# A down-projection in seven products instead of eight, for two of three token blocks

## The chip, the cores and the metric

The kernel runs on one NeuronCore of a Trainium2 chip. The metric is the device time of one execution in microseconds (us). The engines are TensorE (PE: matmuls, with its weight loads as PEld), VectorE (DVE), ScalarE (ACT), GpSimd (POOL) and SyncE (SP), which here only issues DMAs. Matmuls write to PSUM, which has eight banks of 2 KB per partition; a [128 x 512] fp32 tile fills one bank.

## The reference

Sliding-window attention over 4 x 8 heads gives x of 2304 tokens by 512. Two feed-forward layers follow:

```python
a = x @ w_a                       # 512 -> 1536
b = x @ w_b
x = (a * b) @ w_out               # first layer's down-projection, 1536 -> 512
h = x @ w_in                      # 512 -> 2048
g = np.where(h >= 1, h, np.where(h <= -1, 0.0, (h + 1) ** 2 / 4.0))
out = g @ w_out2                  # second layer's down-projection, 2048 -> 512
```

## The kernel before

**Numbers in two parts.** A float32 operand is split into a rounded part (hi) and what is left (lo), both in the type fp32r; a product is three matmuls, hi by hi, hi by lo and lo by hi. ACT makes hi by a copy (L924), DVE makes lo by a subtraction (`minus`, L153).

**Visits.** The tokens lie in three blocks of 768 (`BW`); half a block is 384 (`QW`). After the attention and the first part of the first layer, the work goes in visits (layer, block): a short plain one, then (1,0), (1,1), (1,2), (2,0), (2,1), (2,2). In a visit of the second layer the loop runs over eight pairs of 128-wide feature chunks. For each pair the up-projection is done in seven products of a Strassen scheme (`seven_steps`, L975; q = 0 to 6), six matmuls of 128 x 384 each, into the two banks of the pool `ps_mm`. `bend7` turns their sums into the two chunks of g (`bend`: two ACT passes, a DVE pass at L1018, then hi and lo).

**Down-projection.** For each chunk `down2_pieces` makes six pieces, one for each 128 tokens: three matmuls of 128 x 512 (L1157) that add into one PSUM bank. The six banks (two of the pool `ps_acc`, four of `ps_acc2`) stay open over all sixteen chunks, so that DVE and ACT read them only once, at the end of the visit (L161, L159), before the DMA to `out`.

**Order.** TensorE's order is as the code is written (`MANUAL`). After each product q, `hook` calls `after`, which issues pieces by a rate of 12/7 per hook (`state["credit"]`), while more than `HOLD` = 3 pieces are queued: pieces of a pair run among the products of the next pairs. The other engines' order comes from the framework's scheduler, with the reads of PSUM raised by `urgent()`.

**Weights.** The weights come as 64-bit words. Background jobs (`background`, rates and limits in `BG`) decode them (`words`), form Strassen's combinations for the up-projections (`seven_job`), split them (`staged`) and store them in DRAM. Visits load them from there by SP into 14 tiles of 512 KB (`fill`, L940). `x7_second` prepares the combinations of x for a visit of the second layer, while the visit before it runs.

```python
for k, (m, i) in enumerate(((gh, 0), (gh, 1), (gl, 0))):
    nc.tensor.matmul(
        v["acc"][n], m[:, ss], w[:, i], start=first and k == 0, stop=last and k == 2,
    )
```

Of the kernel before, what the change touches and what calls it, by code (L numbers as in the profile page):

```python
# [26 lines left out]
def attention_and_two_ffns(  # L27
# [631 lines left out]
    for f in range(0, NF2, 2):  # L659
        late += [("ii", f), ("p", f), ("p", f + 1)]  # L660
# [46 lines left out]
    def staged(key, j, src):  # L707
# [12 lines left out]
        minus(V, t[:, 1, :n], src, t[:, 0, :n])  # L720
# [36 lines left out]

    def run(jobs):

        try:  # L760
            return next(jobs[0]) != "no room"
        except StopIteration:
            jobs.popleft()
            return True

    def next_w():
        if not jobs_w and late:
            key = late.popleft()
            jobs_w.append((seven_job if key[0] in ("ab", "ii") else plain_job)(key))
# [27 lines left out]
    def x7_first(b, where):  # L797
# [4 lines left out]
        if where == "memory":  # L802
            parked[b] = {q: dram.tile([P, 2, 2, QW], F32, name=f"t_{b}{q}") for q in (2, 3, 6)}
# [3 lines left out]
        def split(q, c, src):  # L807
# [14 lines left out]
            if q != 4 and where == "memory":  # L822
                nc.sync.dma_start(parked[b][q][:, :, c], t[:, :, :QW].bitcast(F32))
# [37 lines left out]
    def x7_second(b, where):  # L861
# [3 lines left out]
        turned[2, b] = {q: t_tile(where) for q in (2, 3, 6)}  # L865
# [6 lines left out]

        for c in range(2):
# [4 lines left out]
            part = lambda q: [turned[2, b][q][:, z, c] for z in range(2)]  # L878
# [6 lines left out]
            yield from split(*part(3), t1)  # L885
            yield from split(*part(2), t2)
# [5 lines left out]
            yield from split(*part(6), t1)  # L892
# [34 lines left out]
    def fill():  # L927

        while plan:
# [5 lines left out]
            if (key, j) not in wd or room() <= (v < 4):  # L935
# [143 lines left out]
    def down1_pieces(v, f, g):  # L1079
# [29 lines left out]
        return [lambda n=n: go(n) for n in (0, 1, 4, 2, 3, 5)]  # L1109
# [36 lines left out]
    def down2_pieces(v, f, g):  # L1146
# [156 lines left out]
```

## Time and profile before

| what | value |
|---|---|
| median of 3 runs (lowest, highest) | 976.31 us (973.74, 978.48) |
| profiled execution, its span | 976.94 us, 975.2 us |
| PE busy, DVE, ACT, POOL (share of the span) | 96%, 67%, 56%, 13% |
| visits by time in the span (us) | (1,0) 317 to 410, (1,1) to 502, (1,2) to 594.5, (2,0) to 720, (2,1) to 845.4, (2,2) to 971.4 |

Busy time of PE is no measure of its rate, since matmuls overlap in it; the rate is read from the distance between the starts of matmuls that follow one another. The same holds for short instructions of DVE: the listed time of one includes its write at the end, which the next one overlaps.

### The profile page before, as it was taken

The page shows a single profiled execution, that of the slowest core. Times are in us where ns is not written, and L with a number is a line of the kernel's source. Part 1 is how long each engine was busy: PE and PEld are TensorE (multiplying, and loading weights), DVE is VectorE, ACT ScalarE, POOL GpSimd, SP SyncE. Part 2 cuts the span into 40 slices and gives each one's busy share as a digit, 9 for nine tenths or more (in the row PEclk, how much of TensorE's full clock was granted, in tenths as well). Part 3 has the DMA queues.
Part 4 walks back from the last instruction along what each step waited for, and adds up shares of the span by engine and source line. Part 5 has one row for each costly group of instructions (what it writes and reads, how often), then busy time and mean ns, then how long its engine had stood idle before and what let it go on. Part 6 is the DMA issues. An engine that isn't in the chain of part 4 may idle for free.

```text
span 975.2 us, 17548 instructions
## 1 busy us (share of the span) xinstructions
PE 940.9 (96%) x6172; PEld 866.6 (89%) x6172; DVE 651.8 (67%) x1567; ACT 544.4 (56%) x1305; POOL 127.9 (13%) x279
## 2 busy tenths in 40 slices
PE   5999999899999999999999999999999999999998
PEld 4889888889999999999989999989988898989887
DVE  6698788784764989785677667899874333444343
ACT  6778676664433454343444435888775545545453
POOL 4567444344100000000000000000000000000000
PEclk9899999999999999999999999999999999999999
DMA  9966787830435888799868998876876553265521
GB/s 217 187 137 164 219 206 198 217 106 2 154 139 196 318 308 315 279 351 343 268 229 322 387 363 276 312 243 217 300 266 198 188 180 108 82 214 181 184 76 65
DMA packets 172103, 212.44 MB, mean 218 GB/s; under 512 B 92400, under 2 KB 129776, under 8 KB 172016
## 3 DMA queue, kind: packets, MB, share of 16 engines
q1 hardware_dynamic: 168576, 208.44, 66.3%
q10 hardware_dynamic: 3440, 2.88, 0.9%
q8 instruction: 49, 0.80, 0.3%
q14 instruction: 38, 0.31, 0.1%
HBM read 147.06 MB, written 64.23 MB: 217 GB/s over the span
## 4 chain that ended last, share of the span: by engine, by line
PE 71%; DVE 4%; DMA 3%; issue 1%; ACT 0%; SPq 0%; POOL 0%; DVEq 0%; POOLq 0%
PE mm L975 33%; PE acc L1157 20%; PE acc L1096 10%; PE mm L1065 2%; DMA xf<-xf 1%; PE ps_s L331 1%; PE ps_o L395 1%; PE acc L621 1%; PE mm L572 1%; DMA w<-in_moe_w_b_dram 1%; PE mm L574 1%; PE mm L573 1%; DVE x L829 1%; DMA e<-w_b 0%; PE ps_t L363 0%
## 5 line engine op out<-in xcount | busy, mean ns | idle before, releaser
L1157 PE MATMUL acc<-ws,gh 128*128 128x512 f32 x444 | 138.1, 392 | 0.0
L975 PE MATMUL mm<-xt,ws 128*128 128x384 f32 x612 | 123.4, 336 | 0.3 <-DVE a L916 0.3
L975 PEld LDWEIGHTS mm<-xt,ws 128*128 128x128 f32 x612 | 107.4, 188 | 7.3 <-DVE a L916 0.9
L975 PE MATMUL mm<-z,ws 128*128 128x384 f32 x480 | 97.0, 337 | 0.5 <-DVE h L916 0.5
L975 PEld LDWEIGHTS mm<-z,ws 128*128 128x128 f32 x480 | 86.0, 188 | 7.6 <-DVE h L916 0.8
L1157 PEld LDWEIGHTS acc<-ws,gh 128*128 128x128 f32 x444 | 81.6, 188 | 9.3
L1018 DVE SCALAR_TENSOR_TENSOR c<-h,c 128x384 f32<-128x384 f32 x96 | 53.1, 555 | 53.9 <-ACT c L1017 53.7
L1157 PE MATMUL acc<-ws,gl 128*128 128x512 f32 x222 | 88.1, 397 | 0.0
L916 DVE TENSOR_TENSOR h<-mm,s 128x384 f32<-128x384 f32 x72 | 40.0, 556 | 71.0 <-PE mm L975 70.8
L924 ACT CAST gh<-c 128x384 fp32r<-128x384 f32 x96 | 47.8, 512 | 68.2 <-PE acc L1157 65.8
L1016 ACT ACTIVATE c<-h,half 128x384 f32<-128x384 f32 x96 | 59.0, 616 | 26.7 <-DVE gl L153 16.0
L352 POOL TENSOR_SCALAR s<-s,ssum 128x192 f32<-128x192 f32 (+2 forms) x144 | 69.1, 492 | 29.5 <-DVE ssum L347 20.9
L341 ACT ACTIVATE s<-s,nmax 128x192 f32<-128x192 f32 (+2 forms) x144 | 62.6, 439 | 15.5 <-DVE nmax L337 15.1
L153 DVE TENSOR_TENSOR gl<-c,gh 128x384 fp32r<-128x384 f32 x96 | 52.0, 555 | 28.8 <-ACT gh L924 28.5
L975 PE MATMUL mm<-x,ws 128*128 128x384 f32 x348 | 70.4, 336 | 0.4 <-ACT s L996 0.2
L1096 PE MATMUL acc<-gh,ws 128*128 128x512 f32 (+1 forms) x224 | 65.7, 337 | 0.0
L975 PEld LDWEIGHTS mm<-x,ws 128*128 128x128 f32 x348 | 61.7, 188 | 4.0 <-ACT s L996 0.9
L331 PE MATMUL ps_s<-kt,diag 128*128 128x192 f32 (+2 forms) x288 | 62.7, 339 | 2.5 <-DVE nmax L337 1.0
L512 ACT ACTIVATE e<-w 128x512 f32<-128x512 f32 x68 | 45.4, 671 | 35.1 <-DMA w_a<-e 6.3
L924 ACT CAST gh<-a 128x384 fp32r<-128x384 f32 x56 | 28.3, 513 | 55.4 <-DVE a L1004 37.8
L514 ACT ACTIVATE up<-w 128x512 uint32<-128x512 uint32 x68 | 45.9, 675 | 21.5 <-DVE e L525 9.1
L572 PE MATMUL mm<-x,w 128*128 128x256 f32 x192 | 57.2, 302 | 0.2
(126 smaller groups left out, 2223.6 us busy)
## 6 DMA issues: line engine op xcount, KB each, us to landing
ws<-w_ii SPq DMA_DIRECT2D x55, 512.0 KB, 4.2
ws<-w_ab SPq DMA_DIRECT2D x37, 512.0 KB, 6.4
ws<-w_p SPq DMA_DIRECT2D x33, 512.0 KB, 3.7
w<-in_moe_w_out_dram SPq DMA_DIRECT2D x28, 512.0 KB, 4.8
w_ab<-wb SPq DMA_DIRECT2D x24, 512.0 KB, 2.9
w_ii<-wb SPq DMA_DIRECT2D x24, 512.0 KB, 3.5
w<-in_moe_w_in_dram SPq DMA_DIRECT2D x16, 512.0 KB, 4.9
w_p<-wb SPq DMA_DIRECT2D x16, 512.0 KB, 5.3
```

Source lines behind the costliest of these rows:

```text
L153: eng.tensor_tensor(out_, a, hi.bitcast(F32), ALU.subtract)
L331: nc.tensor.matmul(ps[:, z, c : 3 * D], qd[:, i - q0 // D, :], kt[:, (i - 2) * D + c - k0 : (i + 1) * D - k0], start=True, stop=True,)
L341: nc.scalar.activation(at(z, i), at(z, i), AF.Exp, bias=nmax[:, z : z + 1], scale=-1.0, accum_out=ssum[:, z : z + 1],)
L352: ENG[E_N[2 * b + (m >= 2)][z]].tensor_scalar(at(z, i), at(z, i), ssum[:, z : z + 1], 1.0, ALU.mult, ALU.mult)
L514: nc.scalar.activation(up, lo, AF.Copy, scale=2.0**-29)
L572: nc.tensor.matmul(ps, w[:, 0, cs], xh[c], start=(c == 0), stop=False)
L924: nc.scalar.copy(hi[:, t_], src)
L975: nc.tensor.matmul(ps, w[:, k, cs], operand(here, q, ci, m), start=q in (0, 1, 3) and ci + n == 0, stop=ci == 1 and n == 2, skip_group_che ...
L1016: nc.scalar.activation(c, h, AF.Relu, bias=half, scale=0.5)
L1018: V.scalar_tensor_tensor(c, h, 1.0, c, ALU.max, ALU.min)
L1096: nc.tensor.matmul(dst, w[:, i, cs], m[:, t_], start=first and k == 0 and (n < NC or c % 2 == 0), stop=last and k == 2 and (n < NC or c % ...
L1157: nc.tensor.matmul(v["acc"][n], m[:, ss], w[:, i], start=first and k == 0, stop=last and k == 2,)
```

## The change

In the visits (2,1) and (2,2) (`D7`), seven of the eight pairs are projected down by Strassen's scheme, for two chunks by two halves of the tokens by two halves of the 512 outputs. The last pair of each visit is done by the eight plain products, which also close the sums.

- `bend14` takes the place of `bend7`: the curve is applied in place to four halves (a11, a12, a21, a22), POOL forms four combinations of them (`E_C` = 'P'), and all seven operands are split into hi and lo (four halves of 384, twice, were split before).
- `down7_pieces` takes the place of `down2_pieces`: 21 pieces of three matmuls of 128 x 256, three (128 tokens each) for each of seven products, in `ORDER` 0, 6, 3, 1, 2, 5, 4. Products 1, 5 and two thirds of 6 stay in four open PSUM banks; 0, 2, 3, 4 and the rest of 6 go through the two banks of `ps_acc` and are added to sums in SBUF after each pair (`evict`: by ACT in the first pair of a visit, else by DVE). A piece counts 4/7, so three are issued in a hook.
- `close7_pieces` does the last pair: 12 pieces of six matmuls of 128 x 256, then the sums and four DMAs of 384 KB. Before it POOL combines the four sums in SBUF (`E_W`).
- `second_job` makes the weights of the second down-projection: the plain ones as before, and two more tiles for each pair with four combinations (`p7`), by POOL (`E_PC`), stored in DRAM. All weight work ends before (2,1) begins (`last_places`), and `BG` is set so that it runs earlier.
- The x combinations for (2,2) go through DRAM, as those of (1,1) do, and `last_places` gives the freed SBUF to the sums and the operands.

```diff
-    BG = [(3, 2, 24), (3, 1, 24), (1.5, 1, 19), (2, 1, 12), (3, 1, 0), (3, 1, 0), (2, 1, 0)]
+    BG = [(3, 2, 16), (3, 1, 14), (2, 1, 11), (2, 1, 7), (4, 1, 0), (3, 1, 0), (2, 1, 0)]
...
+    def second_job(key):
...
+        yield from staged(("p", f), 0, w[:, 0:2].rearrange("p a n -> p (a n)"))
+        yield from staged(("p", f + 1), 0, low)
+        for dst, i, j in ((t1, b12, b11), (t2, b22, t1), (t3, b22, b12), (t4, b21, t2)):
+            ENG[E_PC].tensor_tensor(dst, i, j, ALU.subtract)
+            yield
+        for j in range(2):
+            yield from staged(("p7", f), j, w[:, 2 + 2 * j : 4 + 2 * j].rearrange("p a n -> p (a n)"), ENG[E_PC])
...
+        def curve(h):
+            c = later["act"].tile([P, QW], F32, tag="c", name="c", bufs=CB)
+            nc.scalar.activation(c, h, AF.Relu, bias=half, scale=0.5)
+            nc.scalar.activation(c, c, AF.Square)
+            V.scalar_tensor_tensor(h, h, 1.0, c, ALU.max, ALU.min)
...
+                elif q == 5:
+                    sub(a22, a21, a22, ALU.add)
+                    sub(a21, a11, a21)
+                    sub(a11, a22, a11)
+                    split(3, a22)
+                    split(4, a21)
+                    split(2, a11)
+                elif q == 6:
+                    split(1, a12)
+                    sub(a12, a12, a11)
+                    split(5, a12)
...
+    ORDER = (0, 6, 3, 1, 2, 5, 4)
...
+        def evict(dst, ps):
+            with urgent(PRI_E):
+                if first:
+                    ecopy(E_F[len(dst.shape) - 2], dst, ps)
+                else:
+                    plus(dst, ps, dst)
...
+            if m < 2:
+                if q in (1, 5, 6):
+                    ps, opens, closes = v["acc"][q], first and m == 0, False
+                else:
+                    if m == 0:
+                        state["bank"] = ps_acc.tile([P, 2, HW], F32, tag="acc", name="acc")
+                    ps, opens, closes = state["bank"], m == 0, True
+                dst = ps[:, m]
+            elif q in (1, 5):
+                dst, opens, closes = v["rest"][:, q // 5], first and q == 1, False
+            else:
+                ps = ps_acc.tile([P, 2, HW], F32, tag="acc", name="acc")
+                dst, opens, closes = ps[:, 0], True, True
+            ss = slice(m * P, (m + 1) * P)
+            for n, (a, b) in enumerate(((0, 0), (0, 1), (1, 0))):
+                nc.tensor.matmul(
+                    dst, g[a][:, ss], w[:, b], start=opens and n == 0, stop=closes and n == 2,
+                    skip_group_check=True,
+                )
+            if m == 1 and q not in (1, 5, 6):
+                evict(v["sum"][q][:, 0:2], state["bank"])
+            if m == 2 and q not in (1, 5):
+                evict(v["sum"][q][:, 0 if q == 6 else 2], dst)
...
+        return [(4 / 7, lambda q=q, m=m: go(q, m)) for q in ORDER for m in range(3)]
```

TensorE before, in (2,2): two hooks of a pair (`mm` are the products of the up-projection, `acc_10184` and the following the six open banks).

```order
L975 MATMUL mm_10941<-xt_8900,ws_10756 128x384 x6
L1157 MATMUL acc_10185<-ws_10683,gh_10841 128x512 x2
L1157 MATMUL acc_10185<-ws_10683,gl_10842 128x512
L1157 MATMUL acc_10186<-ws_10683,gh_10841 128x512 x2
L1157 MATMUL acc_10186<-ws_10683,gl_10842 128x512
L975 MATMUL mm_10993<-xt_8901,ws_10756 128x384 x6
```

TensorE now, in (2,2), after q = 0, 1 and 2 of a pair: `acc_11593` and `acc_11613` are product 4 of the pair before (two thirds, then one third), `acc_11618` is product 0 of the next, all three in the two banks of `ps_acc`.

```order
L1346 MATMUL acc_10837<-ws_11182,go_11341 128x256 x6
L1025 MATMUL mm_11574<-z2_9035,ws_11407 128x384 x3
L1025 MATMUL mm_11574<-z3_9036,ws_11407 128x384 x3
L1346 MATMUL acc_10839<-ws_11182,go_11341 128x256 x3
L1346 MATMUL acc_11593<-ws_11129,go_11307 128x256 x6
L1025 MATMUL mm_11552<-xt_10459,ws_11409 128x384 x6
L1346 MATMUL acc_11613<-ws_11129,go_11307 128x256 x3
L1346 MATMUL acc_11618<-ws_11260,goh_11392 128x256 x2
L1346 MATMUL acc_11618<-ws_11260,gol_11393 128x256
```

Between two products of the up-projection stand now nine matmuls of 128 x 256 where three or six of 128 x 512 stood. In every pair `acc_11618` is the place where a bank is wanted again soonest: it is that of `acc_11593`.

VectorE before, in (2,2), one pair in a row: three sums of products (`h0`, `h1`), four ends of the curve (`c`), four lo parts (`gl`).

```order
L916 TENSOR_TENSOR h0_10574<-mm_10567,s1_10559 128x384
L153 TENSOR_TENSOR gl_10500<-c_10502,gh_10499 128x384
L153 TENSOR_TENSOR gl_10500<-c_10541,gh_10499 128x384
L1018 SCALAR_TENSOR_TENSOR c_10578<-h0_10574,c_10578 128x384
L916 TENSOR_TENSOR h1_10631<-mm_10552,s1_10615 128x384
L153 TENSOR_TENSOR gl_10576<-c_10578,gh_10575 128x384
L916 TENSOR_TENSOR h0_10574<-mm_10608,s2_10600 128x384
L1018 SCALAR_TENSOR_TENSOR c_10635<-h1_10631,c_10635 128x384
L1018 SCALAR_TENSOR_TENSOR c_10653<-h0_10574,c_10653 128x384
L153 TENSOR_TENSOR gl_10576<-c_10653,gh_10575 128x384
L1018 SCALAR_TENSOR_TENSOR c_10674<-h1_10631,c_10674 128x384
```

VectorE now, in (2,2), around the same place as TensorE's piece (`sum4` and `sum0` are the evictions of products 4 and 0, `go` lo parts of operands).

```order
L1236 SCALAR_TENSOR_TENSOR h1_11464<-h1_11464,c_11528 128x384
L966 TENSOR_TENSOR sum2_10832<-acc_11561,sum2_10832 128x256
L166 TENSOR_TENSOR gol_11500<-h1_11464,goh_11499 128x384
L166 TENSOR_TENSOR gol_11500<-h0_11386,goh_11499 128x384
L966 TENSOR_TENSOR h0_11581<-mm_11574,s1_11559 128x384
L166 TENSOR_TENSOR go_11505<-h0_11386,go_11505 128x384
L966 TENSOR_TENSOR sum4_10834<-acc_11593,sum4_10834 128x512
L166 TENSOR_TENSOR go_11532<-h1_11464,go_11532 128x384
L1236 SCALAR_TENSOR_TENSOR h0_11581<-h0_11581,c_11583 128x384
L966 TENSOR_TENSOR sum4_10834<-acc_11613,sum4_10834 128x256
L966 TENSOR_TENSOR sum0_10831<-acc_11618,sum0_10831 128x512
```

Before, nothing in this row frees a bank of the down-projection. Now the evictions that free them stand in the same queue as the curve and the lo parts, and the eviction of `acc_11593` stands behind lo parts whose inputs come from ACT.

## Rows read from the trace of the kernel before

**Rows 1.** Busy time by visit: (1,0), (1,2), (2,0), (2,2); stretch, length, then engines.
```profile
317.00:410.00 93.00, 92.74 (x529) 87.39 (x528) 81.27 (x169) 43.65 (x88) 0.00 (x0) 1.00 0.86 310
502.00:594.50 92.50, 90.87 (x518) 85.81 (x517) 64.07 (x127) 36.78 (x72) 0.00 (x0) 1.00 0.96 356
594.50:720.00 125.50, 125.00 (x630) 112.62 (x629) 111.10 (x224) 99.51 (x200) 0.00 (x0) 1.00 0.75 266
845.40:971.40 126.00, 125.91 (x621) 112.12 (x619) 49.90 (x91) 64.23 (x129) 0.00 (x0) 1.00 0.45 144
```

**Rows 2.** Chain that ended last, in (2,2): start, length, what.
```profile
878.46 1.06 PE mm L975 x6
879.52 1.39 PE acc L1157 x6
...
956.89 1.06 PE mm L975 x6
...
960.39 8.22 PE acc L1157 x36
```

**Rows 3.** Timeline of PE in (1,2): start, length; six matmuls of 128 x 256 between.
```profile
562.96 0.28 PE L1096 MATMUL acc<-gh,ws 128*128 128x256 f32 x1
...
563.67 1.21 PE L975 MATMUL mm<-xt,ws 128*128 128x384 f32 x6
```

**Rows 4.** Groups by line: weight loads and matmuls of L1096, whole span.
```profile
L1096 PEld LDWEIGHTS acc<-gh,ws 128*128 128x128 f32 x224 | 40.0, 188 | 3.0
...
L1096 PE MATMUL acc<-gh,ws 128*128 128x256 f32 x112 | 24.4, 280 | 0.0
```

**Rows 5.** Groups by line, DVE, whole span: busy, mean ns, idle before and releaser.
```profile
L1018 DVE SCALAR_TENSOR_TENSOR c<-h,c 128x384 f32<-128x384 f32 x96 | 53.1, 555 | 53.9 <-ACT c L1017 53.7
L153 DVE TENSOR_TENSOR gl<-c,gh 128x384 fp32r<-128x384 f32 x96 | 52.0, 555 | 28.8 <-ACT gh L924 28.5
...
L916 DVE TENSOR_TENSOR h<-mm,s 128x384 f32<-128x384 f32 x72 | 40.0, 556 | 71.0 <-PE mm L975 70.8
```

**Rows 6.** Groups by line, DVE, 320 to 720 us: PSUM added to sums in SBUF.
```profile
L916 DVE TENSOR_TENSOR xsum<-acc,xsum 128x512 f32<-128x512 f32 x12 | 8.1, 685 | 0.5 <-PE acc L1096 0.4
...
L916 DVE TENSOR_TENSOR xsum<-acc,xsum 128x256 f32<-128x256 f32 x12 | 4.5, 417 | 0.1
```

**Rows 7.** Timeline of DVE, 254.5 to 264 us.
```profile
255.52 0.68 DVE L153 TENSOR_TENSOR wb<-w,wb 128x512 fp32r<-128x512 f32 x1
256.13 1.10 DVE L153 TENSOR_TENSOR xt<-x,xt 128x384 fp32r<-128x384 f32 x1
257.15 0.41 DVE L748 TENSOR_TENSOR w<-w 128x256 f32<-128x256 f32 x1
257.49 0.54 DVE L153 TENSOR_TENSOR xt<-x,xt 128x384 fp32r<-128x384 f32 x1
257.95 0.54 DVE L829 TENSOR_TENSOR x<-x,x 128x384 f32<-128x384 f32 x1
...
262.36 0.90 DVE L153 TENSOR_TENSOR xt<-x,xt 128x384 fp32r<-128x384 f32 x1
```

**Rows 8.** Timeline of POOL, 254 to 264 us.
```profile
255.85 0.95 POOL L153 TENSOR_TENSOR gl<-a_sb,gh 128x256 fp32r<-128x256 f32 x1 [4.41 <-ACT gh L601]
261.83 1.01 POOL L153 TENSOR_TENSOR gl<-a_sb,gh 128x256 fp32r<-128x256 f32 x1 [5.02 <-ACT gh L601]
```

**Rows 9.** POOL's L153: ns min/median/max of one, first and last start.
```profile
L153 POOL TENSOR_TENSOR gl<-a_sb,gh x24: 726/734/1272, 49.6 to 261.8; 128x256 fp32r<-128x256 f32 x24
...
L153 POOL TENSOR_TENSOR w<-e,w x12: 1259/1280/1723, 16.3 to 90.8; 128x512 fp32r<-128x512 f32 x12
```

**Rows 10.** DMA issues: queue, count, KB each, median us to landing.
```profile
t<-wt SPq DMA_DIRECT2D x6, 384.0 KB, 3.7
...
out_dram<-y ACTq DMA_DIRECT2D x9, 256.0 KB, 3.5
```

**Rows 11.** Timeline at the end of the span: DVE's last instruction.
```profile
971.52 0.69 DVE L161 COPY y<-acc 128x512 f32<-128x512 f32 x1 [0.84 <-DMA out_dram<-y]
```

More of the change, by code (lines that the diff above doesn't have):

```diff
@@ L864, in x7_second @@
         xs[b] = [x_tile(f"z{c}") for c in range(NC)]
[L865 removed]
+        if where == "memory":
+            parked[2, b] = {q: dram.tile([P, 2, 2, QW], F32, name=f"t2_{b}{q}") for q in (2, 3, 6)}
+        else:
+            turned[2, b] = {q: t_tile(where) for q in (2, 3, 6)}
         def split(hi, lo, src):
@@ L871, in split, with turn @@
             yield
+        def turn(q, c, src):
+            if where != "memory":
+                yield from split(*(turned[2, b][q][:, z, c] for z in range(2)), src)
+                return
+            while not room():
+                yield "no room"
+            me = ("turned2", b, q, c)
+            take(me)
+            t = w_tile("wt")
+            yield from split(t[:, 0, :QW], t[:, 1, :QW], src)
+            nc.sync.dma_start(parked[2, b][q][:, :, c], t[:, :, :QW].bitcast(F32))
+            give(me)
         for c in range(2):
@@ new lines, in close7_pieces, with go @@
+    def close7_pieces(v, f, got):
+        g, HW = [x for _, x in got], 2 * P
+        s = v["sum"]
+        def go(row, col, m):
+            x = {(0, 0): 1, (0, 1): 5, (1, 0): 6}.get((row, col))
+            fresh = False
+            if x and m < 2:
+                dst = v["acc"][x][:, m]
+            elif x in (1, 5):
+                dst = v["rest"][:, x // 5]
+            elif m < 2:
+                if m == 0:
+                    v["free"] = ps_acc.tile([P, 2, HW], F32, tag="acc", name="acc")
+                dst, fresh = v["free"][:, m], m == 0
+            else:
+                fresh = "odd" not in v
+                if fresh:
+                    v["odd"] = ps_acc.tile([P, 2, HW], F32, tag="acc", name="acc")
+                dst = v["odd"][:, col]
+            ss = slice(row * QW + m * P, row * QW + (m + 1) * P)
+            for k in range(2):
+                w = get(v["at"], ("p", f + k), 0)[:, :, col * HW : (col + 1) * HW]
+                for n, (a, b) in enumerate(((0, 0), (0, 1), (1, 0))):
+                    nc.tensor.matmul(
+                        dst, g[k][a][:, ss], w[:, b], start=fresh and k + n == 0, stop=k == 1 and n == 2,
+                        skip_group_check=True,
+                    )
+            if (row, col, m) == CLOSE[-1]:
+                for k in range(2):
+                    leave(v["at"], ("p", f + k), 0)
+            if m == 0:
+                return
+            z = {(0, 0): 0, (0, 1): 3, (1, 0): 2, (1, 1): 4}[row, col]
+            with urgent():
+                if m == 1:
+                    ps = v["acc"][x] if x else v["free"]
+                    plus(s[z][:, 0:2], ps, s[z][:, 0:2])
+                else:
+                    plus(s[z][:, 2], dst, s[z][:, 2])
+                    if x == 6:
+                        plus(s[z][:, 2], s[6][:, 0], s[z][:, 2])
+                    r = v["b"] * BW + row * QW
+                    ENG["SA"[row]].dma_start(
+                        out[r : r + QW, col * HW : (col + 1) * HW].rearrange("(m p) d -> p m d", p=P), s[z]
+                    )
+        CLOSE = [(row, col, m) for row, col in CORD for m in range(3)]
+        return [(1.0, lambda t=t: go(*t)) for t in CLOSE]
```

192 lines of the change are left out of this document (156 added, 36 removed).

## The prediction

> **What bounds the kernel now.** I read the busy time by visit first. In (2,2) PE is busy for 125.91 of 126.00 us at a granted clock of 1.00 (its upper level, 2.4 GHz), DVE for 49.90, ACT for 64.23, DMA for 0.45 of the time [rows 1]; in (2,0), where the weights' work lies, DVE is at 111.10 of 125.50 and PE still loses only 0.50. Then the chain of waits: in (2,2) it holds nothing but L975 and L1157, matmul behind matmul, until the last 36 [rows 2]. So in the stages that change only matmul time counts, and every wait that PE is given is paid in full.
>
> **What a pair costs PE.** By the chain five pairs take 956.89 - 878.46 = 78.43 us, 15.69 each [rows 2]. The up-projection's seven groups of six take 1.05 each, 7.35; 8.34 is left for 36 matmuls of 128 x 512, 0.232 each. The new shape is 128 x 256, and the first layer has it: six from 562.96 to 563.67, 0.118 each [rows 3]; I take 0.119, between this and the 0.12 that they would have with a little more between them. A pair with Strassen has 7 x 3 x 3 = 63: 7.50 us. It saves 0.84, and 14 pairs save 11.8. The two closing pairs have 72 each, 8.57 against 8.34, and give back 0.5. The term is **-11.3 us** (by 0.118 and 0.121 a matmul -12.3 and -9.3).
>
> The rule to weigh here is one against the change, since matmuls become shorter while each keeps its weight load. In L1096 224 loads stand for 224 matmuls, of which 112 are 128 x 256; a load is listed with 188 ns, longer than the 118 ns from start to start [rows 3, 4]. So the loads pass beside the matmuls, and their number (513 for 288 in a visit) costs nothing. The Trainium skill (TensorE: Matmul & The Clock Gate, section "LDWEIGHTS (loading the stationary operand)", and in Part 3 "The mechanism") gives a load of 128 columns as 128/1.2, 107 ns, and lets it overlap a matmul in flight only where their row groups differ. By that, an estimate from the page, a pair would take 2 us more than before; the spacing in [rows 3] contradicts it.
>
> **What DVE has to do in a pair.** Listed times are 555 ns for 384 columns, 685 for PSUM plus SBUF at 512, 417 at 256 [rows 5, 6], but DVE starts its next instruction earlier: 0.46 after a start at 384 (257.49, 257.95), 0.34 at 256 (257.15, 257.49), 0.61 at 512 (255.52, 256.13) [rows 7]. Now a pair has 3 + 4 + 4 = 11 at 384: 5.1 us. Then it has 3 + 4 + 7 = 14 at 384, four evictions at 512 and five at 256: 6.4 + 2.4 + 1.7 = 10.6 of 14.85 us. That fits; the question is whether each eviction comes in time.
>
> **Where an eviction is awaited.** The two banks of `ps_acc` change hands nine times in a pair. I lay out the order with 1.05 us for a product of the up-projection and 0.357 for three matmuls, 2.12 us from hook to hook. Two thirds of product 4 end 1.41 us before product 0 wants that bank; all other banks have 1.76 to 3.9. The eviction there can start at the last matmul's listed end, 0.16 after its stream (0.28 listed, 0.118 to the next start [rows 3]), and takes 0.69, so DVE may be some 0.5 us late. In front of it stand the curve's ends and lo parts of the last halves [the VectorE order above]. In the layout without any disturbance it starts on time.
>
> **The disturbance is POOL.** Four combinations of 384 run on POOL from the end of a11's and a21's curve on, and on just this stretch. POOL took 0.73 for 256 and 1.28 for 512 when nothing met it [rows 9]; 1.0 for 384 is my estimate between them. Where a POOL subtraction ran from 255.85 to 256.80, a DVE subtraction with both inputs in SBUF, started at 256.13, took 1.10 instead of 0.54, and another 0.90 [rows 7, 8]: 0.36 to 0.56 lost, and the DVE one ends about 0.4 after POOL's. Lo parts and curve ends are such instructions; evictions and sums read PSUM and one tile of SBUF. If each of the four meets one, DVE loses 1.4 to 2.2 us in the 4 us ahead of the critical eviction, has about 1.1 us of idle time there and 0.5 of allowance: PE waits 0 to 0.6 us in a pair. I take 0.3, for 12 pairs (the first of each visit is evicted by ACT): **+3.6 us** (0 to 7; 11 if POOL always goes first, 0.9 a pair).
>
> The Trainium skill (SBUF — State Buffer, "Who interferes with whom") says that a DVE instruction with two SBUF inputs contends with a GpSimd instruction that reads SBUF, and that whoever issues first keeps the shared port while the other blocks. The trace agrees by the 1.10 for 0.54. If POOL always came first, it is the first rival below.
>
> **The other terms.** `x7_second` for block 2 runs in (2,1), no longer beside bare accumulation: by the order some 3.5 us of it (two lo parts of 768 among them) fall into the first pair whose sums DVE evicts. There DVE has 10.6 + 3.5 + 1.6 (POOL) = 15.7 of 14.85: **+0.9** (0 to 3). Weights: 16 more tiles, 8.4 MB, are written before (2,1), and one pair's weights more in (1,0), whose DVE goes from 81 to about 89 of 93 us, while (2,0) is relieved by 6; (1,2) already moves 356 GB/s with 1.6 us of PE lost [rows 1]. PE's order there is unchanged. I take **+0.5** (0 to 5: twice the loss of (1,2), and 2 more in (1,0)). Loads: a pair of (2,1) and (2,2) fetches 3.75 MB, 253 GB/s, less than (1,2) moves; nothing. Change of visit: the sums' tiles wait for the four DMAs of (2,1), issued 4 to 8 us earlier; nothing (0 to 1). The end: the last DVE step is 0.42 instead of 0.69 [rows 6, 11] without the 0.2 that waited for DMA, then 384 KB instead of 256, 3.7 for 3.5 [rows 10], in rows of 1 KB, which no row shows: **+0.3** (-0.4 to 1.5).
>
> **The sum.** -11.3 + 3.6 + 0.9 + 0.5 + 0.3 = -6.0. From the profiled execution, 976.94 (its span 975.2 and 1.7 around it), 970.9; the median of the runs lies 0.6 below that, so 970.3. I say **970.5 us**, with 964.5 to 974 for this case.
>
> **Rivals.**
> - *POOL first.* DVE is held by every POOL combination, 0.9 us a pair at PE, 3 in (2,1), and in earlier visits by the six POOL steps of each `second_job`: -11.3 + 11 + 3 + 1 leaves about 980 at worst, 974 to 980. For it: each of the meetings shown was lost by DVE [rows 7, 8]. Against: POOL's 0.95 and 1.01 there for 0.73 otherwise show that it loses too [rows 9], and evictions are not touched.
> - *Evictions behind ACT (slower).* DVE waited 53.7 us for 96 squares and 28.5 for 96 hi parts, 0.56 and 0.30 each [rows 5], at no cost, since nothing behind them freed a bank of the down-projection. Now evictions stand behind. If a pair's four and seven such waits stay, 2.2 + 2.1 = 4.3 us, DVE needs 10.6 + 1.6 + 4.3 = 16.5 for a pair: 0.8 more than before in 12 pairs, +9.8, less 1.7 in the two first pairs, plus 0.5 and the other terms: about 987. It decides from the point where waits exceed 14.85 - 12.2 = 2.6 us a pair. Against: those waits were mostly DVE with nothing to do (49.90 of 126 busy), and the new order puts other work ahead.
> - *Weight loads not hidden (slower).* A pair has 27 loads more; at 0.188 each, in line with the matmuls [rows 4], 5.1 us, 14 pairs would take 60 us more than before, 1036. The 0.118 from start to start speaks against it [rows 3]. By the page's rule above it would be 2 us a pair, 1004.
> - *Nothing saved*, if a matmul of 256 cost over 0.132 (8.34/63): the row has 0.118.
>
> **How the numbers follow.** Forecast 0.62, POOL first 0.22, evictions behind ACT 0.13, the rest 0.03. A measurement of this kernel tells 0.5%, 4.9 us, from no change: faster is below 971.4, slower above 981.2. Three quarters of the forecast's case are faster, 0.47; its rest and POOL first are the same, 0.37; the other two make 0.16. The range of 8 in 10 is 964.5 to 980.5: below it lies only a forecast without any wait, above it the slower rivals.
>
> **What would show it.** L1346 spaced at 0.118 to 0.121 and a pair at 14.9 to 15.3 in (2,2); PE's waits at L1346 and L975 put down to DVE `sum4`, in total 3 to 8 us; DVE at 100 to 110 of each visit's 120 us by listed time; DVE's lo parts at 0.9 to 1.1 beside POOL. PE waits above 1 us a pair in (2,2), or put down to ACT, would make the prediction wrong; so would waits for DMA in (1,0) to (2,0).

## The result, and the profile after

| | before | changed |
|---|---|---|
| median of 6 runs each, same chip (us) | 976.54 (973.74 to 978.48) | 987.88 (984.04 to 989.68) |
| ratio, 95% interval | | 1.0112 (1.0087 to 1.0138) |
| profiled execution, its span | 976.94, 975.2 | 987.92, 985.4 |
| PE, DVE, ACT, POOL busy (share of the span) | 96, 67, 56, 13% | 95, 78, 58, 27% |

Slower by 1.1%, where 970.5 and at most 980.5 was predicted. Busy time by visit of the changed kernel, cut at the first up-projection matmul of each visit, the last one at the last matmul ((1,0) to (2,2); columns as in [rows 1], whose stretches lie 7 to 11 us later than these visits):

```profile
305.10:399.70 94.60, 93.24 (x530) 88.07 (x529) 77.78 (x162) 46.11 (x92) 0.00 (x0) 1.00 0.82 284
399.70:497.80 98.10, 93.86 (x531) 87.96 (x530) 76.29 (x147) 42.91 (x84) 15.55 (x15) 1.00 0.91 340
497.80:592.20 94.40, 93.55 (x530) 87.95 (x529) 65.69 (x124) 38.41 (x75) 11.61 (x10) 1.00 0.97 356
592.20:718.90 126.70, 124.53 (x616) 111.31 (x615) 112.08 (x201) 94.74 (x193) 29.16 (x24) 0.99 0.76 268
718.90:844.00 125.10, 121.20 (x802) 116.72 (x801) 99.48 (x179) 81.93 (x170) 32.86 (x28) 1.00 0.83 295
844.00:980.80 136.80, 133.65 (x943) 131.87 (x942) 107.93 (x190) 81.40 (x166) 47.32 (x36) 0.99 0.59 195
```

The first four visits of before, cut in the same way:

```profile
306.20:399.50 93.30, 93.04 (x530) 87.69 (x530) 77.32 (x161) 45.41 (x91) 0.00 (x0) 1.00 0.82 293
399.50:492.20 92.70, 92.61 (x530) 87.98 (x530) 66.16 (x133) 36.63 (x72) 0.00 (x0) 1.00 0.89 316
492.20:587.80 95.60, 93.52 (x530) 87.79 (x529) 68.44 (x134) 39.95 (x79) 0.00 (x0) 1.00 0.89 332
587.80:709.90 122.10, 121.60 (x616) 109.79 (x616) 106.48 (x213) 94.02 (x191) 0.00 (x0) 1.00 0.76 270
```

Its other two take 125.5 and 135.5. So the four visits in which nothing was to change, (1,0) to (2,0), went from 403.8 to 413.8, and the two with the new scheme from 261.0 to 261.9. The work ahead of (1,0) was 1.1 shorter, the end 0.3 longer: +10.2, the difference of the spans.

Matmul time is not the reason. The chain of waits in (2,2), every seventh product (start, length, what), answers to [rows 2]:

```profile
900.84 1.05 PE mm L1025 x6
...
915.68 1.04 PE mm L1025 x6
...
930.57 1.05 PE mm L1025 x6
...
939.05 0.69 DVE sum L966
939.75 1.38 DVE h L1236
```

Pairs of 14.84 and 14.89 us, where 14.85 was predicted and 15.69 stood before; and then the chain leaves PE for DVE, as it never did before in (2,2). PE's two largest groups of waits in (2,1) and (2,2) (us in total, times, longest), of 6.6 listed in all, and DVE beside POOL's additions of the sums, at the start of (2,2):

```profile
PE acc L1346 <- DVE sum L966: 3.4, 7, 1.1
PE acc L1390 <- ACT gh L974: 1.3, 1, 1.3
```

```profile
846.19 2.19 DVE L166 TENSOR_TENSOR gl<-c,gh 128x384 fp32r<-128x384 f32 x1
...
849.62 0.88 DVE L1068 SCALAR_TENSOR_TENSOR c<-h,c 128x384 f32<-128x384 f32 x1 [0.77 <-ACT c L1067]
850.42 0.68 DVE L966 TENSOR_TENSOR sum<-acc,sum 128x512 f32<-128x512 f32 x1
...
852.93 1.60 DVE L1068 SCALAR_TENSOR_TENSOR c<-h,c 128x384 f32<-128x384 f32 x1 [0.50 <-ACT c L1067]
854.46 2.18 DVE L1236 SCALAR_TENSOR_TENSOR h<-h,c 128x384 f32<-128x384 f32 x1
```

```profile
846.12 1.84 POOL L1359 TENSOR_TENSOR sum<-sum,sum 128x768 f32<-128x768 f32 x1 [10.62 <-DVE sum L966]
848.04 2.04 POOL L1359 TENSOR_TENSOR sum<-sum,sum 128x768 f32<-128x768 f32 x1
852.11 2.01 POOL L1359 TENSOR_TENSOR sum<-sum,sum 128x768 f32<-128x768 f32 x1 [2.03 <-DVE sum L966]
854.20 2.02 POOL L1359 TENSOR_TENSOR sum<-sum,sum 128x768 f32<-128x768 f32 x1
```

DVE's steps of 0.55 [rows 5] took 2.19, 0.88, 1.60 and 2.18. POOL's additions end at 847.96, 850.08, 854.12 and 856.22, the DVE steps at 848.38, 850.50, 854.53 and 856.64, each 0.41 to 0.42 after one. The addition from PSUM at 850.42 fell between POOL's, and elsewhere such additions keep a mean of 683 ns (below). PE stood still for 1.5 us there (849.62 to 851.09), and then ran for a while at its lower clock level (the third number from the end is the granted clock; 0.50 and 1.00 are its levels, 1.2 and 2.4 GHz):

```profile
851.00:854.50 3.50, 3.29 (x12) 2.80 (x13) 3.00 (x6) 2.90 (x7) 2.31 (x2) 0.67 0.18 70
```

Six matmuls of 384 took 1.92 us there, from 852.87 to the next instruction, for 1.05. The longest wait in (2,0) has the same form, with the weights' work: PE's six matmuls start at 667.64 where the last one before started at 665.38, and are again at the lower level (2.13 for 1.22).

```profile
665.36 1.76 DVE L166 TENSOR_TENSOR wb<-e,wb 128x512 fp32r<-128x512 f32 x1
667.04 0.55 DVE L966 TENSOR_TENSOR h<-mm,s 128x384 f32<-128x384 f32 x1
```

```profile
665.11 3.14 POOL L166 TENSOR_TENSOR wb<-w,wb 128x512 fp32r<-128x512 f32 x2
```

```profile
667.64 2.13 PE L1025 MATMUL mm<-xt,wb 128*128 128x384 f32 x6 [1.85 <-DVE h L966]
```

### The profile page after: what moved, and what is told of

The parts are those of the page before. It is cut to its first block, busy times and chain, and to the rows that moved or that the text cites. A ratio compares the mean times of both kernels' runs of the same rounds, so it can differ in the third digit from the quotient of the medians.

```text
span 985.4 us, 18950 instructions
## 1 busy us (share of the span) xinstructions
PE 938.5 (95%) x6622; PEld 882.5 (90%) x6622; DVE 763.7 (78%) x1729; ACT 576.0 (58%) x1375; POOL 264.4 (27%) x391
## 4 chain that ended last, share of the span: by engine, by line
PE 56%; DVE 13%; ACT 4%; DMA 3%; issue 2%; POOL 1%; SPq 0%; DVEq 0%; POOLq 0%; ACTq 0%
PE mm L1025 26%; PE acc L1146 9%; PE acc L1346 8%; PE acc L1207 4%; PE mm L1115 2%; DMA w_ii<-wb 2%; PE acc L1390 1%; DVE gl L166 1%; DVE wb L166 1%; DVE sum L966 1%; DMA e<-w_b 1%; DVE go L166 1%; PE ps_s L344 1%; POOL h L1251 1%; PE ps_o L408 1%
## 5 line engine op out<-in xcount | busy, mean ns | idle before, releaser
L1025 PE MATMUL mm<-xt,ws 128*128 128x384 f32 x612 | 125.1, 339 | 0.2 <-DVE h L966 0.2
L788 POOL TENSOR_TENSOR w<-w 128x256 f32<-128x256 f32 x8 | 8.1, 1016 | 316.6 <-ACT e L526 217.4
L1251 POOL TENSOR_TENSOR h<-h,h 128x384 f32<-128x384 f32 x42 | 47.5, 1131 | 158.7 <-DVE h L1236 124.1
L1025 PEld LDWEIGHTS mm<-z,ws 128*128 128x128 f32 x480 | 81.8, 188 | 1.5
L1346 PE MATMUL acc<-ws,go 128*128 128x256 f32 x540 | 77.8, 283 | 4.1 <-DVE sum L966 3.2
L1346 PEld LDWEIGHTS acc<-ws,go 128*128 128x128 f32 x540 | 72.3, 189 | 6.6 <-DVE sum L966 5.4
L966 DVE TENSOR_TENSOR sum<-acc,sum 128x512 f32<-128x512 f32 (+1 forms) x124 | 65.5, 537 | 14.9 <-PE acc L1346 10.7
L735 ACT CAST wb<-w 128x512 fp32r<-128x512 f32 x72 | 44.3, 618 | 31.7 <-PE acc L1146 8.1
L589 PE MATMUL mm<-x,w 128*128 128x256 f32 x192 | 57.3, 303 | 1.7 <-ACT x L172 1.6
L591 PE MATMUL mm<-x,w 128*128 128x256 f32 x192 | 56.6, 296 | 0.1
L590 PE MATMUL mm<-x,w 128*128 128x256 f32 x192 | 56.3, 295 | 0.0
```

The source lines that it names most:

```text
L589: nc.tensor.matmul(ps, w[:, 0, cs], xh[c], start=(c == 0), stop=False)
L590: nc.tensor.matmul(ps, w[:, 0, cs], xl[c], start=False, stop=False)
L591: nc.tensor.matmul(ps, w[:, 1, cs], xh[c], start=False, stop=(c == NC - 1))
L966: V.tensor_tensor(out_, ps, sb, ALU.add)
L1025: nc.tensor.matmul(ps, w[:, k, cs], operand(here, q, ci, m), start=q in (0, 1, 3) and ci + n == 0, stop=ci == 1 and n == 2, skip_group_che ...
L1251: ENG[E_C].tensor_tensor(out_, i, j, op)
```

## The experiments

Theory A: POOL's new work holds DVE's steps with two inputs in SBUF. B: DVE's added work and its order behind ACT do it, POOL or not. C: the weights' work costs the earlier visits, by the place where it stands (C1) or by what was added (C2). All results first; visits are from one profiled execution each, medians from the timed runs, the ratio against before on the same chip. One visit can differ between executions with the same work: (1,0) took 93.3 us in before and 94.9 in before_rates, so differences of less than some 1.6 us in a single visit are not read as effects.

| kernel | median | ratio (95%) | (1,0) to (2,0) | (2,1) | (2,2) |
|---|---|---|---|---|---|
| before | 976.54 | | 403.8 | 125.5 | 135.5 |
| changed | 987.88 | 1.0112 (1.0087, 1.0138) | 413.8 | 125.1 | 136.8 |
| no_pool | 981.02 | 1.0022 (1.0003, 1.0042) | 418.4 | 120.2 | 130.9 |
| no_pool_weights | 992.48 | 1.0135 (1.0106, 1.0164) | 418.9 | 124.1 | 136.9 |
| all_dve | 983.21 | 1.0043 (1.0022, 1.0064) | 413.8 | 121.7 | 135.8 |
| sums_dve | 985.52 | 1.0074 (1.0048, 1.0100) | 415.0 | 125.0 | 135.8 |
| d7_none | 989.37 | 1.0122 (1.0097, 1.0148) | 414.3 | 126.6 | 136.8 |
| before_early | 988.22 | 1.0111 (1.0081, 1.0141) | 415.4 | 125.5 | 135.5 |
| late_weights | 996.36 | 1.0194 (1.0166, 1.0223) | 422.3 | 126.0 | 136.2 |
| best1 | 992.23 | 1.0157 (1.0122, 1.0192) | 421.3 | 122.6 | 134.0 |
| half | 986.23 | 1.0081 (1.0051, 1.0110) | 406.7 | 128.7 | 138.8 |
| ops_unread | 1005.14 | 1.0284 (1.0251, 1.0317) | 414.0 | 134.6 | 145.6 |
| before_rates | 976.01 | 0.9983 (0.9964, 1.0002) | 403.6 | 125.5 | 135.5 |
| d7_none_tt2 | 988.8, one run | | 411.7 | 126.6 | 136.8 |
| half2 | 983.72 | 1.0039 (1.0022, 1.0056) | 407.0 | 128.3 | 137.5 |
| early_no_bits | 985.26 | 1.0054 (1.0029, 1.0078) | 412.3 | 125.5 | 135.5 |
| half3 | 979.70 | 1.0022 (1.0002, 1.0042) | 407.1 | 128.1 | 134.1 |

### POOL in the last two visits

**no_pool**

```diff
-            ENG[E_C].tensor_tensor(out_, i, j, op)
+            return
...
-            yield from staged(("p7", f), j, w[:, 2 + 2 * j : 4 + 2 * j]..., ENG[E_PC])
+        yield from staged(("p", f), 0, w[:, 0:2]..., twin=(("p7", f), 0))
...
-                            ENG[E_W].tensor_tensor(s[z], s[y], s[z], ALU.add)
+                        pass
```

> All of POOL's work that the change brought is left out: the plain tiles are stored twice in place of the two tiles of combinations of each pair (same DMA traffic, no subtractions), the four operand combinations of a pair are not formed (the operands are split from what is there), and the sums are not combined before the last pair. ACT's and DVE's other work, all DMAs and TensorE's order stay. Theory A (POOL's instructions with two SBUF inputs hold DVE's, so evictions, sums and lo parts come late and PE waits): PE's gaps in (2,1) and (2,2) fall from 11.2 us to under 4, no stretch of PE at the lower clock there, and with the earlier visits 965 to 972. Theory B (it is DVE's added work and its order behind ACT, whatever POOL does): over 980. Theory C (the weights' work and DMA put earlier cost the earlier visits 9 us, POOL or not): 974 to 980, with (1,1) still at 97 to 98 us against 92.7.

The two visits took 251.1 us, 10.8 less than in the changed kernel and 9.9 less than before; PE's listed waits there are 0.9 us, for 6.6 in the changed kernel. That is what A has for these visits, and it is also nearly the saving that the matmuls were to bring. B falls: DVE's evictions and their order behind ACT are all still there. But with POOL's instructions the waits for their results went too, which ops_unread parts. And the earlier visits became longer, not shorter (418.4), and so the whole was 981.0, not the 965 to 972 that A had.

**ops_unread** parts A: POOL does the same four combinations, but nobody waits for them.

```diff
-            ENG[E_C].tensor_tensor(out_, i, j, op)
+            dump = later["fin"].tile([P, QW], F32, tag="dump", name="dump", bufs=1)
+            ENG[E_C].tensor_tensor(dump, i, j, op)
```

> The changed kernel with POOL's four operand combinations of a pair still done, but into a tile that nobody reads; the operands are split from what is there (so the products are of other operands). Weights and sums as in the changed kernel. It parts theory A in two. A1 (POOL holds the port and DVE's two-input instructions wait): (2,1) and (2,2) stay at 259 to 262 us together, 984 to 988 in all. A2 (what costs is the chain: four POOL steps of 1.13 one behind the other, ahead of the lo parts that DVE has in its order): they fall to 252 to 256, about 978 to 982.

Neither: 280.2 us for the two visits, 18 more than with the chain. DVE's groups in (2,1) (busy, mean ns of one, idle before), of ops_unread:

```profile
L166 DVE TENSOR_TENSOR go<-h,go 128x384 fp32r<-128x384 f32 x29 | 22.1, 778 | 2.7 <-ACT go L1247 2.6
...
L966 DVE TENSOR_TENSOR sum<-acc,sum 128x512 f32<-128x512 f32 x22 | 15.0, 683 | 2.7 <-PE acc L1347 2.7
```

of the changed kernel:

```profile
L1251 POOL TENSOR_TENSOR h<-h,h 128x384 f32<-128x384 f32 x21 | 24.0, 1143 | 86.4 <-DVE h L1236 73.9 <-DVE go L166 7.9 <-DVE gol L166 4.0
L1236 DVE SCALAR_TENSOR_TENSOR h<-h,c 128x384 f32<-128x384 f32 x28 | 18.1, 647 | 8.6 <-ACT c L1235 8.6
L166 DVE TENSOR_TENSOR go<-h,go 128x384 fp32r<-128x384 f32 x29 | 17.8, 620 | 1.1 <-ACT go L1247 0.6
L966 DVE TENSOR_TENSOR sum<-acc,sum 128x512 f32<-128x512 f32 x22 | 15.0, 683 | 1.1 <-PE acc L1346 0.9
```

and of no_pool:

```profile
L166 DVE TENSOR_TENSOR go<-h,go 128x384 fp32r<-128x384 f32 x29 | 15.5, 553 | 2.7 <-ACT go L1245 2.6
L1234 DVE SCALAR_TENSOR_TENSOR h<-h,c 128x384 f32<-128x384 f32 x28 | 15.4, 554 | 9.0 <-ACT c L1233 8.9
L964 DVE TENSOR_TENSOR sum<-acc,sum 128x512 f32<-128x512 f32 x22 | 15.2, 689 | 3.4 <-PE acc L1344 2.9
```

The lo parts of operands (`go`) go from 553 (no_pool) to 620 (changed) to 778 ns, the additions that read PSUM stay at 683 to 689. Counted step by step in both visits, 32 of DVE's steps were stretched (by more than 0.08 us) beside POOL's combinations in the changed kernel, by 17.4 us in all, and 50 in ops_unread, by 32.1. In (2,1) PE waited 11.1 us there for DVE's `sum`. So A2 falls; the rows show A1's cause, but its size was wrong. Why more steps meet POOL is argued, not shown: without the wait for POOL's results the lo parts are free to run beside it.

**all_dve** and **sums_dve** leave nothing out.

```diff
-    E_C = 'P'
+    E_C = 'V'
...
-    E_PC = 'P'
-    E_W = 'P'
+    E_PC = 'V'
+    E_W = 'V'
```

> POOL's three kinds of work (weights' combinations, operands' combinations, combining of the sums) are done by DVE, so that nothing is left out and nothing shares the port. By listed times DVE gets 4 x 0.55 = 2.2 us more in a pair (10.6 + 2.2 = 12.8 of 14.9) and 16 x 3.3 = 26 us (some 4 of 256, 2 of 512) in the stages of the weights. Theory A: (2,1) and (2,2) fall to about 121 and 131 us (they were 125.1 and 136.8), while (1,0) and (1,1), where DVE is at 83 of 95 already, may get longer: 976 to 984 in all. Theory B: (2,1) and (2,2) become longer by DVE's added work, above 990.

> Only the combining of the sums before each last pair (four additions of 128x768, listed with 1.98 us each on POOL, 8 us in (2,1) and 8 in (2,2)) goes from POOL to DVE. Theory A: the stretches at 846 and 852 us, in which DVE's lo parts beside these additions took 2.19, 1.60 and 2.18 us instead of 0.55 and after which PE ran at about 1.2 GHz, and the gaps at 944 and 973, are gone: 2 to 5 us faster than the changed kernel, 983 to 986. Theory B: DVE gets 4 us more in two pairs that are full, so 988 to 990.

all_dve: 983.2 is in A's range. (2,1) took 121.7, nearly as A has it and 3.4 less than with the combinations on POOL, though DVE is busier (102.92 for 99.48): on DVE a combination is listed with 552 ns, on POOL with 1143, in which it can hold DVE. (2,2) missed, 135.8 for 131: the eight additions of the sums now stand on DVE, four of them at the change of visit (its first pair took 19.6 us, 19.2 in the changed kernel). Even so the two visits took 257.5, 3.5 less than before, with nothing left out. sums_dve is in A's range too, 985.5, and no DVE step of 2 us is left; its two visits are 1.1 us shorter than the changed kernel's, but its interval overlaps that of the changed kernel, so a gain is not shown.

### The place of the weights' work

**no_pool_weights** (only the combined weights' making left out) and **d7_none** (`D7 = ()`).

> Only the making of the combined weights is left out: the plain tiles are stored twice in their place, so the DMA traffic stays, while four subtractions of 256 and two of 512 on POOL and two copies of 512 on ACT for each pair go. POOL's operand combinations and its combining of the sums stay. Theory A: (1,1) and (2,0) give back most of the 5.4 and 4.6 us by which they became longer, (2,1) and (2,2) stay: 978 to 982. Theory B: (1,1) and (2,0) give back only the part that ACT's copies held: 983 to 987. Theory C (DMA and the earlier place of the work): no change, 986 to 989.

> The changed kernel with no visit done by the new scheme: (2,1) and (2,2) are projected down as before, while all weights, the combined ones too, are made, stored and placed as in the changed kernel (their tiles are then not used). Theory C (the earlier visits lose by what was done to the weights, whatever the last two do): (1,0) to (2,0) take 412 to 415 us against 403.8 before, (2,1) and (2,2) 125.5 and 135.5, 983 to 987 in all. Rival (the earlier visits lose because the last two need something of them): 976 to 979.

In no_pool_weights (2,0) came back from 126.8 to 122.7. But (1,1) stayed at 97.6, and (1,2) rose from 94.4 to 103.0: a job has fewer steps without the combinations, the steps are issued at the same rate, so the jobs stand elsewhere. By the traces DVE has 77 steps for the weights in (2,0) for 89 in the changed kernel, and 52 for 40 in (1,2). So what POOL's steps for the weights cost in (2,0) is not shown apart. All three theories missed the sum; the place came out as a suspect. d7_none has C in the visits, 414.3 with the last visits done as before; its 989.4 lies above the 983 to 987.

**before_early**: the kernel before, nothing added.

```diff
-    BG = [(3, 2, 24), (3, 1, 24), (1.5, 1, 19), (2, 1, 12), (3, 1, 0), (3, 1, 0), (2, 1, 0)]
+    BG = [(3, 2, 24), (3, 1, 21), (2, 1, 17), (2, 1, 11), (4, 1, 0), (3, 1, 0), (2, 1, 0)]
```

> The kernel before with one edit: its limits of the weights' work are set so that the jobs stand in the same visits as in the changed kernel (one pair of the second layer's weights in (1,0), one and a half in (1,1), two in (1,2), the rest in (2,0)); no job is added. Theory C1 (the place of the work is the cost: DVE's steps for the weights meet those for x of the next visit in (1,1)): (1,1) 96 to 98 us, 981 to 985 in all. Theory C2 (the added tiles are the cost: ACT's copies, POOL's subtractions, 8.4 MB more): 976 to 979.

415.4 for the four visits, 11.7 more than before, with not one tile added; (1,1) as C1 has it, the whole above C1's 981 to 985. C2 falls. Its visits:

```profile
304.00:398.40 94.40, 93.04 (x529) 87.74 (x529) 78.27 (x163) 46.65 (x93) 0.00 (x0) 1.00 0.82 286
398.40:494.70 96.30, 94.42 (x530) 87.63 (x529) 74.31 (x151) 41.57 (x83) 0.00 (x0) 1.00 0.92 346
494.70:593.70 99.00, 95.29 (x530) 89.26 (x529) 65.44 (x128) 38.33 (x75) 0.00 (x0) 0.98 0.89 317
593.70:719.40 125.70, 121.93 (x617) 109.76 (x616) 100.82 (x200) 91.16 (x182) 0.00 (x0) 1.00 0.75 259
```

The sum is near the changed kernel's 413.8, the places are not: against before the visits lose 1.2, 3.6, 3.4 and 3.6 us here, and 1.3, 5.4, -1.2 and 4.6 in the changed kernel. And DVE has fewer steps for the weights than before in (1,2) and (2,0), 45 for 52 and 80 for 93, where it loses. DVE is at 66 to 83% of these visits, and yet PE waits. One of the waits, in (2,0), DVE and PE:

```profile
610.03 0.56 DVE L879 TENSOR_TENSOR x<-xf 128x384 f32<-128x384 f32 x1 [1.24 <-DMA xf<-xf]
...
616.23 0.56 DVE L916 TENSOR_TENSOR h<-mm,s 128x384 f32<-128x384 f32 x1
```

```profile
616.84 1.31 PE L975 MATMUL mm<-xt,ws 128*128 128x384 f32 x6 [2.40 <-DVE h L916]
```

DVE stood still for data of x until 610.03 (1.24 us); from there on its steps follow one another without a gap. The sum `h` of products that PE had done by 613.1 was read at 616.23, and PE waited 2.4 us for its bank.

**before_rates** (`BG` with before's limits and the changed kernel's rates: 2 for 1.5 in (1,1), 4 for 3 in (2,0)) and **late_weights** (the changed kernel with `BG = [(3, 2, 16), (3, 1, 16), (1.5, 1, 13), (2, 1, 8), (4, 1, 0), ...]`).

> The kernel before with its own limits for the weights' work, so that each visit gets the same jobs, but issued at the changed kernel's rates (2 steps a hook in (1,1) for 1.5, 4 in (2,0) for 3). If the pace within a visit is the cost: (1,1) 94 to 96 us, (2,0) 124 to 126, 980 to 985. If it is the place (which visit has the job): 975 to 978.

> The changed kernel with its weights' work put as late as before (none of the second layer's in (1,0), two pairs less one in (1,1), up to four by the end of (1,2), four in (2,0)); all added work stays, on POOL as in the changed kernel. Theory C1: (1,0) and (1,1) fall back to 93.3 to 94 and 93 to 95; (2,0) gets half a pair more and loses up to 3; 980 to 984. Theory C2: the sum of the four visits stays at 412 to 415, 986 to 989.

The pace costs nothing (403.6). Later is no way out for the changed kernel either: (1,0) and (1,1) fell to 94.3 and 93.9 as C1 has it, but (2,0), in which DVE is already busy for 106.48 of 122.10 before, took 136.7, with one wait of 4.6 us behind ACT's `wb`. Both theories missed the whole. The work stands even later here than before (115 of DVE's steps for the weights in (2,0), for 93), so this run does not part what was added from its place either.

**early_no_bits**: before_early without three of DVE's five decoding steps.

> The kernel before with its weights' jobs placed as early as in the changed kernel, and with three of DVE's five steps for the decoding of each weight tile left out from (1,0) on (limits, shift, sign; the weights come out wrong), 1.3 us of DVE a tile; ACT's steps, the combinations, lo parts and all DMAs stay. If the earlier visits lost by DVE's queue (steps for weights and x ahead of the lo parts and sums that PE waits for): they fall from 414.6 to 404 to 409 us, 977 to 982 in all. If they lost by what DVE waits for (ACT's copies, DMAs, room for tiles): 412 to 415, 985 to 989.

Only (1,1) came back (93.4 for 96.3); (1,2) and (2,0) stayed at 98.3 and 125.0 (99.0 and 125.7). So DVE's own steps are the cost in (1,1), and by elimination what DVE waits for in the other two: in (2,0) data of x by DMA, 5.1 us here and 6.5 in before_early, none before. Which transfer or copy holds which wait was not taken apart further.

**best1** (late weights, operands' combinations on DVE, the sums on DVE in thirds without precedence):

> The changed kernel with three edits: the weights' work as late as before, the operands' combinations on DVE, and the sums before the last pair combined on DVE in thirds and without precedence over the rest. Theory A with C1: (2,1) and (2,2) take 121 and 132 us, the earlier visits 404 to 408, 966 to 974 in all, faster than both. If C1 falls, 976 to 980; if A falls, above 982.

(2,1) near what was expected, 122.6, and (2,2) 2 over it, so the two take 4.5 us less than before; the earlier visits lose as in late_weights, 421.3, which C1 had not foreseen, and the whole missed its range by far.

### A version without the early weights

**half** uses the scheme in (2,2) alone and makes the combined weights in (2,1). Beside the lines shown, `E_C` and `E_PC` are 'V' and `BG` puts the other weights' work where it stood before.

```diff
-    D7 = ((2, 1), (2, 2))
+    D7 = ((2, 2),)
...
-    late += [("ii", f), ("pp", f)]
+    late += [("ii", f), ("p", f), ("p", f + 1)]
+    late += [("p7", f) for f in range(0, NF2 - 2, 2)]
```

> The changed kernel with the new scheme in (2,2) alone, so that the combined weights need not be there before (2,2): they are made in (2,1), where DVE was busy for 55 of 125 us, from the plain values stored once more in DRAM; the other weights' work stands where it stood before the change, the combinations of operands and weights are on DVE, the combining of the sums on POOL. If the place of the weights' work is what the earlier visits lost by: they take 404 to 408 us (before 403.8, changed 413.8), (2,1) 125.5 to 128, (2,2) about 131 (before 135.5), 970 to 977 in all, so level with or better than before and over 10 better than the changed kernel. If the added tiles themselves were the cost: 983 or more.

The earlier visits: 406.7, 2.9 more than before, of which 2.2 in (1,0). Both the early place and the added tiles are gone from them, so C1 fits, but this run does not part it from C2. And (2,2) took 138.8: its first seven pairs 105.3 (15.04 each), the rest 33.5 for 25.7 before. There, DVE and POOL:

```profile
964.02 2.15 DVE L1070 SCALAR_TENSOR_TENSOR c<-h,c 128x384 f32<-128x384 f32 x1
966.75 1.51 DVE L166 TENSOR_TENSOR gl<-c,gh 128x384 fp32r<-128x384 f32 x1 [0.58 <-ACT gh L976]
968.18 2.17 DVE L1070 SCALAR_TENSOR_TENSOR c<-h,c 128x384 f32<-128x384 f32 x1
970.93 0.56 DVE L166 TENSOR_TENSOR gl<-c,gh 128x384 fp32r<-128x384 f32 x1 [0.58 <-ACT gh L976]
```

```profile
961.63 8.31 POOL L1361 TENSOR_TENSOR sum<-sum,sum 128x768 f32<-128x768 f32 x4 [700.11 <-DVE sum L968]
```

The four additions take 2.01 to 2.03 each and end at 963.65, 965.76, 967.84 and 969.94; three DVE steps end 0.41 to 0.42 after the last three, and the next, after the fourth, takes 0.56 again. The Trainium skill (SBUF — State Buffer, "Who interferes with whom") says that the engine which issues first keeps the shared pair of ports for its whole instruction while the other blocks. These rows agree: DVE lost what was left of POOL's instruction, up to 1.6 us each time.

**half2** puts these additions on DVE, in thirds and at the start of the last pair's down-projection, and issues the weights' work at other rates; **half3** also gives the curve four buffers for two and leaves the weights' work out of the first pair of (2,1).

```diff
-    E_W = 'P'
+    E_W = 'V'
...
-    CB = 2
+    CB = 4
```

> The kernel with the new scheme in (2,2) alone once more, with three edits: the four sums are combined on DVE, in thirds, at the start of the last pair's down-projection and without precedence (on POOL they took 8.31 us, in which two steps of DVE's curve took 2.15 and 2.17 and PE stood still for 4.0); the weights' work of (1,1) and (2,0) is issued at 2 and 4 steps a hook; the combined weights at 1.5 a hook in (2,1). If POOL's additions were what the end lost by: the last stretch, from the eighth pair on, falls from 33.46 to 26 to 28 us, (2,2) to 131 to 133, and the whole to 974 to 980, level with before. If DVE's 4 us of additions hold the last curve in their place: 980 to 984.

> The kernel with the new scheme in (2,2) alone, with two edits more: four buffers for the curve instead of two (in the last pair ACT waited for DVE's lo parts to free them, and PE stood still for 3.7 us behind that chain), and no weights' work in the first pair of (2,1), where the evictions of (2,0) were late by 1.6 us. If that chain is what the end loses by: the stretch from the eighth pair on falls from 32.1 to 26 to 28 us, (2,2) to 131 to 133, (2,1) to 126.6, and the whole to 974 to 978, level with before or a little faster. If the end is held by DVE's additions themselves: (2,2) stays at 136 to 138, 980 to 984.

half2: the last stretch took 32.1 us and the whole 983.7, as the second theory has it. PE still stood for 3.7 us at the end: with two buffers the curve's first step on ACT waits until DVE has done a lo part, and DVE's additions stand between. half3 took 28.7 for the last stretch and 134.1 for (2,2), 1.4 less than before and just above what was expected, its longest waits 1.3 and 1.6 for DVE's `gl`. (2,1) stayed at 128.1. At 1.0022 (1.0002 to 1.0042) it is the nearest to before of the versions of the new scheme that leave nothing out; none of them was faster than before.

**d7_none_tt2** (d7_none with `TT = 2`):

> The changed kernel with no visit done by the new scheme, and with two tiles of the tag t as before the change instead of three. In the changed kernel six matmuls of 128 x 384 of the up-projection stand 0.1768 us apart in (2,0), before 0.1752, with nothing else changed about them; without the new scheme that stays to the end, with it it is 0.1748 once SBUF is given out anew for (2,1). If the place of tiles in SBUF makes it: 0.1752 with two tiles. If not: 0.1768.

Still 0.1768; the place of these tiles is not it.

## Why the prediction was wrong, point by point

- **PE's term, -11.3: right.** Pairs of 14.84 and 14.89 for 14.85, and no_pool gains 9.9 with 0.9 of listed waits left.
- **"The disturbance is POOL", +3.6 (0 to 7; 11 if POOL always goes first): mis-sized.** It measured 10.8 (no_pool). The mechanism and the instructions that it hits were right, and so were two of the sizes. The 32 steps of DVE that were stretched beside the 56 combinations lost 0.54 us each, 1.24 a pair, where 1.4 to 2.2 was expected; and PE lost 0.34 a pair against no_pool in eleven ordinary pairs, where 0.3 was chosen. What failed is that 0.3 was taken for 12 pairs alike. The second and third pairs of (2,1), where POOL meets the steps of x, lost 3.6 us. The first pair of (2,2), at whose start the sums are added, lost 2.9, and the end 0.6: I had priced these additions at nothing, and did not reckon with the lower clock after the longest waits (granted 0.67 for 3.5 us). The rival "POOL first" came near the 10.8 by 0.9 in each of 12 pairs, which is not where it was lost; that is luck.
- **The weights, +0.5 (0 to 5): the step that failed most.** It measured +10.0. I added DVE's and DMA's time per visit, found both under the visit's length, and took the loss of (1,2) twice. The shift itself was misjudged too: DVE was to get 8 us more in (1,0) and 6 less in (2,0); its busy time rose by 0.5 and 5.6 there, and by 10.1 in (1,1). Moving the jobs earlier is enough for a loss of this size: before_early has 11.7 with nothing added, half, with the jobs where they were and no combined weights made in these visits, 2.9. How the 10.0 of the changed kernel divide between the place, the added steps (POOL's among them) and about 1 us of wider matmul spacing (last section) stays open, since its visits lose in other places than those of before_early.
- Either term alone would have left the time inside the range (970.5 + 7.2 or + 9.5, at most 980.5); both together took it out.
- **`x7_second`, +0.9:** in no_pool the second and third pairs of (2,1) took 15.11 and 14.75 (changed: 16.05 and 17.41). What was lost there came with POOL, and is in its 10.8.
- **The end, +0.3:** 0.28 measured.
- **Evictions behind ACT, 987:** the time came near, the mechanism did not. In the changed kernel 2.6 of PE's 6.6 us of listed waits are put down to ACT; with POOL out, DVE behind the same ACT steps leaves 0.3. **Weight loads not hidden, nothing saved:** refuted by the pairs.
- The sum by what was measured: -9.9 + 10.8 for the two visits, +10.0 for the weights, +0.3 for the end, -1.1 ahead of (1,0): 10.1 for the 10.2 by which the span grew.

## What to carry to other kernels

A helper on POOL is not free beside a full DVE: each of its instructions can hold a DVE step with two SBUF inputs until it ends, so its price is up to its own length, paid on DVE, and the visit was shorter with the combinations on DVE itself (121.7) than on POOL (125.1). The price per meeting was foreseen here; what was missed is the places where POOL meets other work of DVE: the steps of x and the change of visit. Work that is hidden in other stages must be priced by where it stands in the order of an engine and among its waits, not by that engine's busy share (66 to 83% in before_early). Move such jobs alone first, with nothing added: here that one edit cost 1.1%, as much as the whole change.

## What the runs showed of the hardware that was not expected

- In every kernel made from the changed source, six matmuls of 384 stand 0.1755 to 0.1760 us apart in (1,0) to (1,2) and 0.1764 to 0.1768 in (2,0); in those made from before it is 0.1748 to 0.1751 and 0.1753, with the same matmuls in the same order. A pair of the second layer takes 15.82 for 15.69, in d7_none in fifteen of sixteen pairs (the last includes the end), some 1 us in a visit of the second layer and 0.1 to 0.2 in one of the first. With the new scheme's pairs it is 0.175 again. Neither POOL (no_pool), nor the place of the weights, nor the tiles of the tag t make it; it stays open.
- A DVE step of 384 held by POOL ended 0.41 to 0.42 us after POOL's instruction, in seven of seven cases named above, though the step itself takes 0.55.
